# Attention scores as products over 128 rows, with zeros beside each head's queries

## The chip, the cores and the metric

The kernel runs on one core of a Trainium2 chip. Its engines work side by side and meet at semaphores: TensorE (PE in the profile; PEld is its weight load), VectorE (DVE), ScalarE (ACT), GpSimd (POOL), and SyncE (SP), which issues most transfers. The metric is the device time of one execution in microseconds (us); before the change the median of three runs is 1227.53 us (1225.55 to 1228.27).

## The reference

Attention with 32 of 576 scores kept per row, then a routed mixture of eight experts, then a last pair of layers with a leaky activation. The change touches only the first line of the attention:

```python
# q, k, v: 4 batches x 8 heads x 576 rows x 64
scores = scale * np.matmul(q, k.transpose(0, 1, 3, 2))
kth = np.partition(scores, -32, axis=-1)[..., -32:-31]
scores = np.where(scores >= kth, scores, -1000000000.0)
attn = softmax(scores)                    # rows of 576, 32 of them not zero
x = np.matmul(attn, v)                    # then experts and the last layers
```

## The kernel before

The attention takes the first 520 us or so. Heads are worked in 16 pairs (4 batches x 4), and a pair in nine tiles of 128 query rows: jobs j = 0 to 3 are the first 512 rows of the first head, 4 to 7 those of the second, and job 8 holds the last 64 rows of both. With all inputs at two heads of 64 columns side by side, a transposed tile `qk` has the first head on partitions 0 to 63 and the second on 64 to 127, 576 columns of q and 576 of k.

`tile_scores` multiplies a tile of queries (the weights, `qs`) with all 576 keys in two products of 288 columns, each of which TensorE runs as two matmuls (f32), so four per tile. For jobs 0 to 7 queries and keys are the 64 partitions of one head. For job 8 the queries are `qm`, 128 x 128, with the first head's last rows in the upper left quarter, the second head's in the lower right, and zeros elsewhere; the product then runs over all 128 partitions and yields 64 rows of each head.

The tiles go through a software pipeline, written out by hand in `ORDER`: in step i the kernel issues the transposes of tile i-6 (`st_transpose`, into `pt`), the product of tile i+1 (`st_scores`, into the only `s`), and the weighted sum of tile i-7 (`st_out`, into `po`) on TensorE; the evacuation of the transposes (`pT`), the copy of the scores out of `s` (`st_copy`, into one of seven `ss` buffers), the signs of tile i-1 against a threshold (`st_sign1`, `sg`, two buffers) and the exponential of tile i-2 on ScalarE; seven block maxima and the selection of the largest on VectorE; z = scores x signs (`st_z`, two buffers) and the mask (`st_mask`, L288 and L289, `pen`, four buffers) on GpSimd. VectorE reads z two steps after GpSimd made it. Every engine works its own list strictly in order.

While a pair is worked, the next one is prepared in the steps with j = 1, 3 and 5: `prep` transposes 96 rows at a time into a bank of `pt`, `prep_copy` copies 384 columns to `qk` on ScalarE, and after the second copy SP places the two quarters of `qm` by two transfers. For the very first pair `prep_all` does all three at once, before anything else can run. After a batch's last pair VectorE and TensorE route its rows to experts, and some steps later GpSimd scatters them with five indirect transfers (L751); after the last batch the expert weights, whose loading starts near the end of the attention, are multiplied.

Of the kernel before, what the change touches and what calls it, by code (L numbers as in the profile page):

```python
# [12 lines left out]
F32 = mybir.dt.float32  # L13
F32R = mybir.dt.float32r
BF = mybir.dt.bfloat16
I32 = mybir.dt.int32
AF = mybir.ActivationFunctionType
# [4 lines left out]
P = 128  # L22
B, H, S, D = 4, 8, 576, 64
# [3 lines left out]
CK = 116  # L27
NCK = 5
HALF = S // 2
# [16 lines left out]
class Job:  # L46


    def __init__(self, n, b, hp, j, st):
        self.n, self.b, self.hp, self.j, self.st = n, b, hp, j, st  # L50
        self.pre = None

    t = property(lambda self: self.st[self.b * NPAIR + self.hp])
# [3 lines left out]
class Attention:  # L57
    def __init__(self, ctx, tc, q, k, v, sb, ident):
        self.tc, self.nc = tc, tc.nc
        self.q, self.k, self.v = q, k, v  # L60
        self.ident = ident
        nc = self.nc
        self.wk = ctx.enter_context(tc.tile_pool(name="attn", bufs=2))
        self.ps = ctx.enter_context(tc.tile_pool(name="attn_ps", bufs=1, space=PSUM))
        one = ctx.enter_context(tc.tile_pool(name="attn_one", bufs=1))

        self.new_pt1()
        self.new_po()
        self.new_s()

        self.bank = self.ps.tile([P, 512], F32, name="own")
        self.taken = 0
        self.vt = []
        for i in range(3):
            t = one.tile([CK, NCK, 2, D + 1], F32, name=f"vt{i}")
            nc.gpsimd.memset(t, 0.0)
            nc.gpsimd.memset(t[:, :, :, D:D + 1], 1.0)
            self.vt.append(t)
        self.qm = []
        for i in range(2):  # L80
            t = one.tile([P, P], F32, name=f"qm{i}")
            nc.gpsimd.memset(t, 0.0)
            self.qm.append(t)
        self.scores, self.exps = [[one.tile([P, NCK * CK], F32, name=f"{nm}{i}") for i in range(n)]
                                  for nm, n in (("ss", 7), ("e", 5))]
        for t in self.scores + self.exps:
            nc.vector.memset(t[:, S:], 0.0)
        self.identb = one.tile([P, P], BF, name="identb")
        nc.vector.tensor_copy(self.identb, ident)
        vsel = one.tile([P, 9, 2], F32, name="vsel")  # L90
        nc.gpsimd.iota(vsel, pattern=[[2, 9], [1, 2]], base=S - 2 * TOP, channel_multiplier=0,
                       allow_small_or_imprecise_dtypes=True)
        nc.vector.memset(vsel[:, 0, 1:2], -float(S + 1))
        self.vsel = self.own(18).rearrange("p (a b) -> p a b", b=2)
        nc.vector.tensor_copy(self.vsel, vsel)
        self.rden = self.own(6)
        self.fac = self.own(2)
        self.least = self.own(3)
        nc.vector.memset(self.fac[:, 0:1], -0.125)
        nc.vector.memset(self.fac[:, 1:2], TINY)  # L100
        self.bad = sb.tile([P, 1], F32, name="bad")
        nc.vector.memset(self.bad, 0.0)
        self.per = NPAIR * 9
# [41 lines left out]
    def prep(self, t, g):  # L145

        if g == 0:
            t["qk"] = self.wk.tile([P, 2 * S], F32, name="qk", bufs=2)
        pt = self.ps.tile([P, 4, P], F32, name="pt0", bufs=2)
        pt = pt.rearrange("p a b -> p (a b)")[:, :384]  # L150
        for r in range(4):
            i, c = divmod(4 * g + r, 6)
            self.nc.tensor.transpose(pt[:, r * 96:(r + 1) * 96],  # L153
                                     t["qn" if i == 0 else "kn"][:, c].rearrange("p h d -> p (h d)"),
                                     self.ident[:96, :96])
        t["pp"] = pt

    def prep_copy(self, t, g):
        self.nc.scalar.activation(t["qk"][:, g * 384:(g + 1) * 384], t["pp"], AF.Copy)
        if g == 1:  # L160
            t["qm"] = self.qm[t["i"] % 2]
            for h in range(2):
                hs = slice(h * D, (h + 1) * D)
                self.nc.sync.dma_start(t["qm"][hs, hs], t["qk"][hs, S - D:S])

    def tile_scores(self, t, j):
        nc = self.nc
        s = self.new_s()
        h, c0 = divmod(j, 4)
        hs = slice(h * D, (h + 1) * D) if j < 8 else slice(0, P)  # L170
        qs = t["qk"][hs, c0 * P:(c0 + 1) * P] if j < 8 else t["qm"]
        for g in range(2):
            nc.tensor.matmul(s[:, g, :HALF], qs, t["qk"][hs, S + g * HALF:S + (g + 1) * HALF], start=True, stop=True)  # L173
        return s

    def st_scores(self, T):
# [73 lines left out]

    def new_pen(self, T):

        T.pen = self.wk.tile([P, NCK, CK + 4], BF, name="pen", bufs=4)[:, :, :CK]
        return T.pen

    def st_sign2(self, T):
# [6 lines left out]

    def st_sign1(self, T):
        nc, wk = self.nc, self.wk
        T.sg = wk.tile([P, S], F32, name="sg", bufs=2)
        T.c1 = wk.tile([P, 1], F32, name="c1", bufs=5)
        nc.scalar.activation(T.sg, T.ss, AF.Sign, bias=T.w[:, 23:24], scale=-ABOVE, accum_out=T.c1)  # L268

# [4 lines left out]

    def st_z(self, T):
        nc, wk = self.nc, self.wk
        T.z = wk.tile([P, S], F32, name="z", bufs=2)
        eng = nc.vector if T.n >= self.n - self.LASTZ else nc.gpsimd
        eng.tensor_tensor(T.z, T.ss, T.sg, op=OP.mult)  # L279

# [100 lines left out]
    def prep_all(self, t):  # L381
        for g in range(3):
            self.prep(t, g)
            self.prep_copy(t, g)

    def tiles(self, jobs, first, pair_done, batch_done, drain):

# [67 lines left out]
E, FF, FF2, DM = 8, 1024, 2048, H * D  # L455
# [20 lines left out]
class Router:  # L476
# [160 lines left out]
    def batch_done(self, b):  # L637

        nc, wk = self.nc, self.wk
        xs = [(P, self.xb[b][:, j]) for j in range(4)] + [(TAIL, self.xt[b][:, :])]  # L640
        n, t0 = BT, b * BT
# [5 lines left out]
        g, rr = self.narrow  # L647
        lx = new("lg", E)
        ss, r, m, fm = new("ss"), new("rn"), new("mrow"), new("fm")
# [51 lines left out]

        def square(t):
            k, x = xs[t]
            d = self.att.wk.tile([P, S], F32, name="sg", bufs=2)[:k, :DM]
            if t < 2:
                v.scalar_tensor_tensor(d, x[:, :DM], 1.0, x[:, :DM], op0=OP.mult, op1=OP.mult, accum_out=ss[:k, t:t + 1])
            else:
                nc.scalar.activation(d, x[:, :DM], AF.Square, accum_out=ss[:k, t:t + 1])
# [18 lines left out]
        if b == B - 1:  # L727
            low = [lambda f=f: self.low_half(f) for f in range(AHEAD)]
            ahead = lambda at: [lambda f=f: self.ahead(f) for f in range(AHEAD) if AT[f] == at]
            steps += [lambda t=t: square(t) for t in range(4)] + [low[f] for f in range(AHEAD) if AT[f] == 0] + ahead(1) + [  # L730
                lambda: self.last_dots(3), numbers] + ahead(2) + [last_copies, root] + first + [
                counts] + [low[f] for f in range(AHEAD) if AT[f] == 1] + norm + [exps] + ahead(3) + [
                low[f] for f in range(AHEAD) if AT[f] == 2] + [place]
            steps += [x for y in zip(where, sums) for x in y] + [low[f] for f in range(AHEAD) if AT[f] == 3]
        else:
            for t in range(n):
                steps += [("st_transpose", lambda t=t: tile_dots(t)), ("late", lambda t=t: tile_copy(t)),
                          ("late", lambda t=t: tile_norm(t))]
            mixed = [x for y in zip(where, norm) for x in y]
            steps += first + [NEXT, root, ("st_transpose", counts), ("late", place), NEXT] + mixed + [  # L740
                NEXT, exps, NEXT] + sums[:2] + [lambda: (gates(), numbers())]
# [904 lines left out]
```

## Time and profile before

| what | value |
|---|---|
| median of three runs | 1227.53 us |
| profiled execution, device time | 1226.84 us |
| its span | 1225.0 us |
| TensorE busy | 1192.3 us (97%) |
| VectorE, ScalarE, GpSimd busy | 834.1, 689.4, 684.1 us |
| mean granted clock of TensorE | 0.988 of full speed |

The span is what the profile shows of that execution, from its first to its last instruction. Busy time is the union of an engine's instructions; since they overlap at their ends, the start of one instruction to the start of the next says what it holds the engine for. "Idle before" names the event that ended an engine's idle time; "issue" is time for which nothing that the profile shows was waited for.

### The profile page before, as it was taken

To read this page: it belongs to the slowest core of one execution; us is meant where nothing else is said; L and a number is where in the kernel's file an instruction comes from. 1 tells how busy PE (TensorE), PEld (TensorE's weight loads), DVE (VectorE), ACT (ScalarE), POOL (GpSimd) and SP (SyncE) were. 2 spreads that over 40 slices of the span, in tenths; PEclk is the share of its full clock that TensorE was granted. 3 is DMA by queue.
4 is the path that set the end of the run, shared out by engine and by line. 5 is a ranking of instruction groups with operands and counts; after the bars stand their busy time and mean duration, and the time that the engine had idled before them with its cause. 6 is when DMAs were issued, how large, how long until landed. Compare 5 with 4: busy or idle time off the path is not lost.

```text
span 1225.0 us, 24804 instructions
## 1 busy us (share of the span) xinstructions
PE 1192.3 (97%) x8273; PEld 1059.4 (86%) x8273; DVE 834.1 (68%) x3636; ACT 689.4 (56%) x1475; POOL 684.1 (56%) x731
## 2 busy tenths in 40 slices
PE   7999999999999999998999999989999999999996
PEld 4888888888888888898999999979898898998995
DVE  5888888988798889866555566667657664454440
ACT  5899988999799979853544555522323222122120
POOL 4777777988789767951434345445335352333331
PEclk9999999999999999988999999989999999999999
DMA  4333222222222110438877787342232122222211
GB/s 134 96 102 101 57 56 55 83 69 56 56 73 54 33 32 14 149 111 172 211 202 217 187 240 234 112 133 84 69 118 73 54 67 70 78 61 76 73 42 55
DMA packets 121775, 121.24 MB, mean 99 GB/s; under 512 B 73454, under 2 KB 91374, under 8 KB 121638
## 3 DMA queue, kind: packets, MB, share of 16 engines
q1 hardware_dynamic: 118198, 109.58, 32.5%
q0 software_dynamic: 2912, 9.46, 2.1%
q8 instruction: 67, 1.10, 0.4%
q14 instruction: 70, 0.57, 0.2%
q10 hardware_dynamic: 528, 0.52, 0.1%
HBM read 84.58 MB, written 33.92 MB: 97 GB/s over the span
## 4 chain that ended last, share of the span: by engine, by line
PE 94%; DMA 2%; DVE 2%; ACT 1%; issue 1%; POOL 0%; SPq 0%; POOLq 0%; DVEq 0%
PE po L333 14%; PE s L173 14%; PE mm L1023 12%; PE mm L1024 12%; PE mm L1022 12%; PE pt L310 6%; PE mm L1245 5%; PE mm L1244 5%; PE mm L1243 5%; PE pt L312 2%; PE pt L153 2%; PE pt L616 1%; DMA yt<-y 1%; PE pt L596 1%; PE xt L1014 1%
## 5 line engine op out<-in xcount | busy, mean ns | idle before, releaser
L195 DVE MAX8 cand<-ss 128x8 f32<-128x82 f32 (+1 forms) x1008 | 233.3, 232 | 59.7 <-ACT ss L185 59.3
L1023 PE MATMUL mm<-xT,wt 128*128 128x256 f32 (+7 forms) x852 | 248.9, 292 | 4.4 <-DVE xT L1017 4.3
L1022 PE MATMUL mm<-xT,wt 128*128 128x256 f32 (+7 forms) x852 | 247.6, 291 | 5.5 <-ACT xT L1188 5.5
L279 POOL TENSOR_TENSOR z<-ss,sg 128x576 f32<-128x576 f32 x143 | 201.8, 1412 | 91.1 <-ACT sg L268 75.6
L1024 PE MATMUL mm<-xT,wt 128*128 128x256 f32 (+7 forms) x852 | 248.2, 291 | 0.0
L333 PEld LDWEIGHTS po<-vt,pT 116*128 116x128 f32 x1440 | 174.1, 190 | 32.4 <-issue 23.9
L333 PE MATMUL po<-vt,pT 116*128 116x130 f32 x1440 | 194.8, 281 | 0.6 <-ACT pc L365 0.6
L1228 POOL TENSOR_TENSOR hT<-xr,hT 128x256 fp32r<-128x256 f32 x144 | 106.3, 743 | 152.4 <-ACT hT L1227 145.5
L1227 ACT ACTIVATE hT<-xr 128x256 fp32r<-128x256 f32 x144 | 59.0, 416 | 200.9 <-DVE xr L1224 194.0
L173 PE MATMUL s<-qk 64*128 64x288 f32 x512 | 166.3, 447 | 3.8 <-ACT ss L185 3.2
L1022 PEld LDWEIGHTS mm<-xT,wt 128*128 128x128 f32 x852 | 162.9, 191 | 6.5 <-ACT xT L1188 5.7
L1023 PEld LDWEIGHTS mm<-xT,wt 128*128 128x128 f32 x852 | 163.2, 191 | 5.6 <-DVE xT L1017 4.5
L1024 PEld LDWEIGHTS mm<-xT,wt 128*128 128x128 f32 x852 | 163.8, 192 | 0.0
L310 PE MATMUL pt<-ident,e 128*116 128x128 f32 x720 | 129.5, 275 | 1.2 <-POOL e L285 1.2
L1223 DVE TENSOR_SCALAR xr<-mm,alpha 128x256 f32<-128x256 f32 x144 | 69.4, 482 | 84.3 <-PE mm L1024 83.3
L185 ACT ACTIVATE ss<-s 128x576 f32<-128x576 f32 x144 | 94.2, 654 | 55.8 <-PE s L173 53.7
L173 PEld LDWEIGHTS s<-qk 64*128 64x128 f32 x512 | 89.6, 194 | 39.7 <-ACT ss L185 7.0
L947 POOL TENSOR_TENSOR wt<-raw,wt 128x1024 fp32r<-128x1024 f32 x29 | 76.3, 2633 | 83.0 <-ACT wt L946 78.3
L268 ACT ACTIVATE sg<-ss,w 128x576 f32<-128x576 f32 x144 | 111.7, 776 | 0.3 <-DVE w L208 0.2
L273 ACT ACTIVATE e<-ss,sm 128x576 f32<-128x576 f32 x144 | 111.2, 772 | 0.0
L217 DVE MAX8 w<-z 128x8 f32<-128x576 f32 x144 | 106.8, 742 | 2.3 <-POOL z L279 1.8
L312 PE MATMUL pt<-identb,pen 128*116 128x128 bf16 x560 | 99.5, 220 | 0.2 <-POOL pen L289 0.2
(254 smaller groups left out, 2666.7 us busy)
## 6 DMA issues: line engine op xcount, KB each, us to landing
raw<-in_moe_w SPq DMA_DIRECT2D x60, 512.0 KB
xr<-yt SPq DMA_DIRECT2D x17, 512.0 KB
xs<-zeros SPq DMA_DIRECT2D x8, 1028.0 KB
raw<-in_moe_w_in SPq DMA_DIRECT2D x16, 512.0 KB
raw<-in_moe_w_out SPq DMA_DIRECT2D x16, 512.0 KB
yt<-zeros SPq DMA_DIRECT2D x8, 704.0 KB
rows<-in_q SPq DMA_DIRECT2D x32, 144.0 KB
rows<-in_k SPq DMA_DIRECT2D x32, 144.0 KB
```

What stands on the lines that cost most here:

```text
L173: nc.tensor.matmul(s[:, g, :HALF], qs, t["qk"][hs, S + g * HALF:S + (g + 1) * HALF], start=True, stop=True)
L195: blocks.append(lambda i=i: nc.vector.max(A.cand[:, i], A.ss[:, i * BW:(i + 1) * BW if i + 1 < KB else S]))
L217: fin = [lambda: nc.vector.max(C.w[:, 24:32], C.z), lambda: nc.vector.scalar_tensor_tensor(scr, self.vsel, C.c1, C.w[:, 23:32, None].to_br ...
L268: nc.scalar.activation(T.sg, T.ss, AF.Sign, bias=T.w[:, 23:24], scale=-ABOVE, accum_out=T.c1)
L273: nc.scalar.activation(T.e[:, :S], T.ss, AF.Exp, bias=T.sm[:, 0:1], scale=0.125)
L279: eng.tensor_tensor(T.z, T.ss, T.sg, op=OP.mult)
L310: nc.tensor.matmul(o, e, self.ident, is_transpose=True, start=True, stop=not pen)
L312: nc.tensor.matmul(o, T.pen[:, c], self.identb, start=False, stop=True)
L333: nc.tensor.matmul(po[:, i:i + 2, :], T.pT[:, c], rhs, start=(c == 0), stop=(c == NCK - 1))
L1022: nc.tensor.matmul(ps, wh, xh, start=first, stop=False)
L1023: nc.tensor.matmul(ps, wh, xl, start=False, stop=False)
L1024: nc.tensor.matmul(ps, wl, xh, start=False, stop=last)
```

## The change

The queries are laid out with zeros. `qz` (two buffers, 128 x 1152, cleared once) holds in columns 0 to 575 the first head's queries on partitions 0 to 63, and further right the second head's on 64 to 127, its last 64 rows in columns 576 to 639 and the other 512 from column 640 on. Any 128 columns that a job takes are then one head's queries with zeros beside them, or, for job 8 (columns 512 to 639), the two quarters. All products of scores run over 128 partitions, against a `kt` with the keys of both heads. q goes to a staging tile `qt` first, from which three transfers fill `qz`; for the first pair (`direct`) ScalarE copies the first head's part straight from the transposes, and VectorE the second head's. z overwrites the signs, `sg` has three buffers in place of two and two, `ss` has six in place of seven, and `pen` three in place of four.

```diff
@@ -76,13 +76,15 @@
             nc.gpsimd.memset(t, 0.0)
             nc.gpsimd.memset(t[:, :, :, D:D + 1], 1.0)
             self.vt.append(t)
-        self.qm = []
+
+
+        self.qz = []
         for i in range(2):
-            t = one.tile([P, P], F32, name=f"qm{i}")
+            t = one.tile([P, 2 * S], F32, name=f"qz{i}")
             nc.gpsimd.memset(t, 0.0)
-            self.qm.append(t)
+            self.qz.append(t)
         self.scores, self.exps = [[one.tile([P, NCK * CK], F32, name=f"{nm}{i}") for i in range(n)]
-                                  for nm, n in (("ss", 7), ("e", 5))]
+                                  for nm, n in (("ss", 6), ("e", 5))]
         for t in self.scores + self.exps:
             nc.vector.memset(t[:, S:], 0.0)
         self.identb = one.tile([P, P], BF, name="identb")
@@ -145,7 +147,9 @@
     def prep(self, t, g):
 
         if g == 0:
-            t["qk"] = self.wk.tile([P, 2 * S], F32, name="qk", bufs=2)
+            t["q"] = self.wk.tile([P, S], F32, name="qt", bufs=1)
+            t["k"] = self.wk.tile([P, S], F32, name="kt", bufs=2)
+            t["qz"] = self.qz[t["i"] % 2]
         pt = self.ps.tile([P, 4, P], F32, name="pt0", bufs=2)
         pt = pt.rearrange("p a b -> p (a b)")[:, :384]
         for r in range(4):
@@ -155,22 +159,36 @@
                                      self.ident[:96, :96])
         t["pp"] = pt
 
-    def prep_copy(self, t, g):
-        self.nc.scalar.activation(t["qk"][:, g * 384:(g + 1) * 384], t["pp"], AF.Copy)
-        if g == 1:
-            t["qm"] = self.qm[t["i"] % 2]
-            for h in range(2):
-                hs = slice(h * D, (h + 1) * D)
-                self.nc.sync.dma_start(t["qm"][hs, hs], t["qk"][hs, S - D:S])
+    SECOND = ((0, S - D, S + D), (S - D, S, D))
+
+    def prep_copy(self, t, g, direct=False):
+        nc = self.nc
+        for x, o in (("q", 0), ("k", S)):
+            lo, hi = max(g * 384, o), min((g + 1) * 384, o + S)
+            if lo >= hi:
+                continue
+            src = t["pp"][:, lo - g * 384:hi - g * 384]
+            if x == "q" and direct:
+                nc.scalar.activation(t["qz"][:D, lo:hi], src[:D], AF.Copy)
+                for a, b, to in self.SECOND:
+                    a, b = max(a, lo), min(b, hi)
+                    if a < b:
+                        nc.vector.tensor_copy(t["qz"][D:, to + a:to + b], src[D:, a - lo:b - lo])
+            else:
+                nc.scalar.activation(t[x][:, lo - o:hi - o], src, AF.Copy)
+        if g == 1 and not direct:
+            nc.sync.dma_start(t["qz"][:D, :S], t["q"][:D])
+            for a, b, to in self.SECOND:
+                nc.sync.dma_start(t["qz"][D:, to + a:to + b], t["q"][D:, a:b])
 
     def tile_scores(self, t, j):
         nc = self.nc
         s = self.new_s()
         h, c0 = divmod(j, 4)
-        hs = slice(h * D, (h + 1) * D) if j < 8 else slice(0, P)
-        qs = t["qk"][hs, c0 * P:(c0 + 1) * P] if j < 8 else t["qm"]
+        q0 = c0 * P + h * (S + D) if j < 8 else S - D
+        qs = t["qz"][:, q0:q0 + P]
         for g in range(2):
-            nc.tensor.matmul(s[:, g, :HALF], qs, t["qk"][hs, S + g * HALF:S + (g + 1) * HALF], start=True, stop=True)
+            nc.tensor.matmul(s[:, g, :HALF], qs, t["k"][:, g * HALF:(g + 1) * HALF], start=True, stop=True)
         return s
 
     def st_scores(self, T):
@@ -250,7 +268,7 @@
 
     def new_pen(self, T):
 
-        T.pen = self.wk.tile([P, NCK, CK + 4], BF, name="pen", bufs=4)[:, :, :CK]
+        T.pen = self.wk.tile([P, NCK, CK + 4], BF, name="pen", bufs=3)[:, :, :CK]
         return T.pen
 
     def st_sign2(self, T):
@@ -263,7 +281,7 @@
 
     def st_sign1(self, T):
         nc, wk = self.nc, self.wk
-        T.sg = wk.tile([P, S], F32, name="sg", bufs=2)
+        T.sg = wk.tile([P, S], F32, name="sg", bufs=3)
         T.c1 = wk.tile([P, 1], F32, name="c1", bufs=5)
         nc.scalar.activation(T.sg, T.ss, AF.Sign, bias=T.w[:, 23:24], scale=-ABOVE, accum_out=T.c1)
 
@@ -274,7 +292,7 @@
 
     def st_z(self, T):
         nc, wk = self.nc, self.wk
-        T.z = wk.tile([P, S], F32, name="z", bufs=2)
+        T.z = T.sg
         eng = nc.vector if T.n >= self.n - self.LASTZ else nc.gpsimd
         eng.tensor_tensor(T.z, T.ss, T.sg, op=OP.mult)
 
@@ -381,7 +399,7 @@
     def prep_all(self, t):
         for g in range(3):
             self.prep(t, g)
-            self.prep_copy(t, g)
+            self.prep_copy(t, g, True)
 
     def tiles(self, jobs, first, pair_done, batch_done, drain):
 
@@ -701,7 +719,7 @@
 
         def square(t):
             k, x = xs[t]
-            d = self.att.wk.tile([P, S], F32, name="sg", bufs=2)[:k, :DM]
+            d = self.att.wk.tile([P, S], F32, name="sg", bufs=3)[:k, :DM]
             if t < 2:
                 v.scalar_tensor_tensor(d, x[:, :DM], 1.0, x[:, :DM], op0=OP.mult, op1=OP.mult, accum_out=ss[:k, t:t + 1])
             else:
```

Per engine the order of the tiles stays as it was. It changes in two places.

At the start, ScalarE's first rows before (the transposes of the first pair lie in three banks, `pt_154`, `pt_160`, `pt_168`):

```order
L159 ACT_TABLE_LOAD
L159 ACTIVATE qk<-pt_154 128x384 [waits PE_49]
L159 ACTIVATE qk<-pt_160 128x384 [waits PE_49]
L159 ACTIVATE qk<-pt_168 128x384 [waits PE_49]
L185 ACTIVATE ss_109<-s 128x576 [waits PE_49]
```

And after (the banks are now `pt_153`, `pt_160`, `pt_169`):

```order
L172 ACT_TABLE_LOAD [waits PE_49]
L172 ACTIVATE qz_105<-pt_153 64x384 [waits Pool_49]
L172 ACTIVATE qz_105<-pt_160 64x192 [waits PE_49]
L178 ACTIVATE kt<-pt_160 128x192 [waits DVE_49]
L178 ACTIVATE kt<-pt_169 128x384 [waits PE_49]
L203 ACTIVATE ss_109<-s 128x576 [waits PE_49]
```

There is one copy more, the wait for TensorE stands ahead of the table load, and the copy of k waits for VectorE. VectorE's rows in the same place, after:

```order
L95 MEMSET vsel 128x1 [waits Pool_49]
L97 COPY own<-vsel 128x18 [waits DVE_49]
L101 MEMSET own 128x1 [waits DVE_49]
L102 MEMSET own 128x1 [waits DVE_49]
L104 MEMSET bad 128x1
L176 COPY qz_105<-pt_153 64x384 [waits Activation_49]
L176 COPY qz_105<-pt_160 64x128 [waits Activation_49]
L176 COPY qz_105<-pt_160 64x64
L514 TENSOR_SCALAR rev<-iota 128x8 [waits Pool_49]
```

The three copies stand between the constants (`vsel`, which GpSimd makes after its clearings) and the rest; before, `rev` followed `bad` at once. On TensorE the third group of the first pair's transposes waits for these copies, where it waited for ScalarE's first copy:

```order
L157 MATMUL pt_160<-ident,rows 128x96 [waits DMAHW3_49,DMAHW2_49]
L157 MATMUL pt_160<-ident,rows 128x96
L157 MATMUL pt_169<-ident,rows 128x96 [waits DVE_49]
L157 MATMUL pt_169<-ident,rows 128x96 x3
L191 MATMUL s<-kt,qz_105 128x288 [waits Activation_49,Pool_49]
L191 MATMUL s<-kt,qz_105 128x288
```

In the preparation of each later pair, SP's rows before, with the loads of the pair after next behind them:

```order
L164 DMA qm_107<-qk 64x64 [waits DMAHW6_49,Activation_49]
L164 DMA qm_107<-qk 64x64 [waits DMAHW7_49]
L132 DMA rows<-in_q 96x6x64 [waits DMAHW0_49,PE_49]
L132 DMA rows<-in_q 96x6x64 [waits DMAHW1_49]
L132 DMA rows<-in_k 96x6x64 [waits DMAHW2_49]
```

And after:

```order
L180 DMA qz_107<-qt 64x576 [waits DMAHW4_49,Activation_49]
L182 DMA qz_107<-qt 64x512 [waits DMAHW5_49]
L182 DMA qz_107<-qt 64x64 [waits DMAHW6_49]
L134 DMA rows<-in_q 96x6x64 [waits DMAHW7_49,PE_49]
L134 DMA rows<-in_q 96x6x64 [waits DMAHW0_49]
```

Three transfers stand where two were, the first two of them with 576 and 512 columns in place of 64.

## Rows read from the trace of the kernel before

**Rows 1.** The page: busy time, the chain that ended last, one costly group.

```profile
PE 1192.3 (97%) x8273; PEld 1059.4 (86%) x8273; DVE 834.1 (68%) x3636; ACT 689.4 (56%) x1475; POOL 684.1 (56%) x731
...
PE 94%; DMA 2%; DVE 2%; ACT 1%; issue 1%; POOL 0%; SPq 0%; POOLq 0%; DVEq 0%
...
L217 DVE MAX8 w<-z 128x8 f32<-128x576 f32 x144 | 106.8, 742 | 2.3 <-POOL z L279 1.8
```

**Rows 2.** Stretches: length, then busy us of PE, PEld, DVE, ACT, POOL; clock; DMA.

```profile
66.68:97.04 30.36, 30.36 (x225) 25.07 (x224) 26.36 (x173) 27.96 (x63) 24.20 (x26) 1.00 0.37 102
...
224.00:258.00 34.00, 34.00 (x253) 28.32 (x252) 29.73 (x199) 31.46 (x71) 31.41 (x37) 1.00 0.32 92
...
465.00:505.00 40.00, 40.00 (x288) 32.57 (x289) 38.30 (x250) 36.74 (x82) 33.36 (x40) 1.00 0.28 102
```

**Rows 3.** Line 173, the scores: count, ns min/median/max, first and last start, form.

```profile
L173 PE MATMUL s<-qk x512: 402/403/847, 7.4 to 505.5; 64*128 64x288 f32 x171
...
L173 PE MATMUL s<-qk,qm x64: 406/406/848, 34.9 to 509.0; 128*128 128x288 f32 x64
```

**Rows 4.** TensorE in time, jobs 7, 8 and 0: start, us, instruction.

```profile
63.47 1.23 PE L173 MATMUL s<-qk 64*128 64x288 f32 x4
64.63 1.39 PE L333 MATMUL po<-vt,pT 116*128 116x130 f32 x10
65.85 0.27 PE L310 MATMUL pt<-ident,e 128*116 128x128 f32 x1
...
66.63 0.22 PE L312 MATMUL pt<-identb,pen 128*116 128x128 bf16 x1
66.68 1.19 PE L173 MATMUL s<-qk,qm 128*128 128x288 f32 x4
67.71 1.28 PE L333 MATMUL po<-vt,pT 116*128 116x130 f32 x10
68.83 0.27 PE L310 MATMUL pt<-ident,e 128*116 128x128 f32 x1
...
69.60 0.22 PE L312 MATMUL pt<-identb,pen 128*116 128x128 bf16 x1
69.75 1.23 PE L173 MATMUL s<-qk 64*128 64x288 f32 x4
```

**Rows 5.** Waits from 40 to 505 us: total, times, longest.

```profile
PEld po L333 <- issue: 23.5, 61, 0.4
```

**Rows 6.** All engines in time, 254 to 258 us.

```profile
254.48 0.75 POOL L288 TENSOR_SCALAR mg<-ss,nk 128x580 f32<-128x580 f32 x1
...
255.81 0.65 ACT L185 ACTIVATE ss<-s 128x576 f32<-128x576 f32 x1
...
257.12 0.76 ACT L273 ACTIVATE e<-ss,sm 128x576 f32<-128x576 f32 x1
...
257.78 0.58 ACT L317 ACTIVATE pT<-pt 116x512 f32<-116x512 f32 x1
```

**Rows 7.** All engines in time, the start.

```profile
0.82 1.28 ACT L159 ACT_TABLE_LOAD   x1 [0.82 <-PEq L1631]
...
2.82 0.64 POOL L76 MEMSET vt<- 116x650 f32 x1
...
3.56 0.35 POOL L82 MEMSET qm<- 128x128 f32 x2
...
4.73 0.06 DVE L102 MEMSET bad<- 128x1 f32 x1
...
5.15 0.49 ACT L159 ACTIVATE qk<-pt 128x384 f32<-128x384 f32 x1 [3.04 <-PE pt L153]
...
5.62 1.20 PE L153 MATMUL pt<-ident,rows 96*128 96x96 f32 x6 [0.18 <-DMA rows<-in_k]
...
7.39 2.28 PE L173 MATMUL s<-qk 64*128 64x288 f32 x4 [0.58 <-ACT qk L159]
```

**Rows 8.** SP's queue in time: the transfers that place the queries.

```profile
55.59 1.16 SPq L164 DMA_DIRECT2D qm<-qk  x2
```

## The prediction

> **What bounds the kernel now.** Read the page's busy shares and its chain of waits first [rows 1]: TensorE is busy for 97% of the span and makes up 94% of the chain that ends last. A busy TensorE need not be TensorE at its peak, so the next view is the stage that the change touches: the 30.36 us in which one pair of heads passes, from one product with `qm` (66.68 us) to the next (97.04 us) [rows 2]. There TensorE is without a gap, ScalarE has 27.96 us of work, VectorE 26.36 and GpSimd 24.20. TensorE sets the pace, but ScalarE stands only 2.40 us behind. Two other stretches of the same view have less room: the 34 us after a batch's routing (GpSimd 31.41 of 34), and the last 40 us of the attention (VectorE 38.30 of 40) [rows 2].
>
> Now TensorE alone, tile by tile. The kernel already holds both forms of the product: 512 matmuls on 64 rows and 64 on 128 rows, the latter with zeros beside each head's queries [rows 3]. One matmul of either takes the same time, 403 against 406 ns. What differs is what stands around it. Follow the starts in [rows 4]. A tile on 64 rows: product at 63.47, first weighted sum (`po`) at 64.63, first transpose (`pt`) at 65.85; that is 1.16 + 1.22 = 2.38 us. The tile on 128 rows: 66.68, 67.71, 68.83; that is 1.03 + 1.12 = 2.15 us. And the product starts 0.05 us after the last transpose when it is on 128 rows (66.63 to 66.68), 0.15 us when on 64 (69.60 to 69.75). In all 0.23 + 0.10 = 0.33 us per tile. The waits name the same spot: the weight load of `po` is held 0.4 us, 61 times, by "issue", that is by nothing that another engine does [rows 5].
>
> **The gain on TensorE.** The 512 matmuls are 128 tiles of four. In the first pair a matmul takes up to 847 ns (the other form is still at 848 in the first pair's ninth tile, from 34.9 us) [rows 3], and there each product waits for the copy of the one before, so I count nothing for its eight tiles. 120 x 0.33 = 39.6 us. A pair would take 30.36 - 8 x 0.33 = 27.72 us.
>
> **What ScalarE gives back.** Its work in a pair is 27.96 us as shown, 0.24 more than TensorE would then need; over the 12 pairs without routing that is 2.9 us. But busy time counts an instruction's tail: e starts at 257.12 and takes 0.76, yet the next instruction starts at 257.78, after 0.66 [rows 6]. Where ScalarE stops to wait, some 8 times a pair, that tenth is no work; 27.96 - 0.8 = 27.2 us, below TensorE's 27.72. A new cost comes on top: of the three copies of q and k in a pair the second is split in two, for which the row's tail of 0.10 us is an upper end (1.5 us in 15 pairs). I take 1.4 us lost for all this; the ends are 0 and 4.4.
>
> **What GpSimd gives back.** After the routing of batch 0 and of batch 1 GpSimd also scatters rows and is full for some ten tiles [rows 2]. TensorE would pass these 10 x 0.33 = 3.3 us sooner; GpSimd can't. One score buffer less bites here: ScalarE's copy of scores into a buffer must follow GpSimd's last read of the tile six back, not seven. In [rows 6] that read (L288) ends at 254.48 + 0.75 = 255.23 and the copy that would wait for it starts at 255.81: 0.58 us of room. Beyond it ScalarE waits, and behind that copy on its queue are the signs and the exponential, for which GpSimd's next z and then VectorE wait. TensorE needs the copy only for its next product: in [rows 4] a product ends at 66.68 + 1.19 = 67.87, a copy takes 0.65 [rows 6], the next product starts at 69.75, so TensorE has 1.23 us of its own, 0.9 at the new pace. 3.3 - 0.6 - 0.9 = 1.8 us per batch, 3.6 for two; the ends are 1.8 (VectorE's and ScalarE's room absorbs half) and 5.4 (TensorE's slack is already used up).
>
> **What VectorE gives back.** From 465 to 505 us VectorE has 1.7 us left [rows 2], while 11 tiles on 64 rows would save 3.6 us. At least 1.9 us stay lost; I take 2.1 (ends 1.9 and 3.6).
>
> **The start.** Two things make the first product later. ScalarE's table load (1.28 us at 0.82, when nothing waited) now has the wait for TensorE's first transposes ahead of it, so it starts where the first copy started, at 5.15, and the copy (0.49) ends near 6.92 [rows 7]. And VectorE has three new copies of head 1's queries. GpSimd clears two `qz` of 1152 columns instead of two `qm` of 128: 650 columns take 0.64 us and the two of 128 together 0.35 [rows 7], which makes 0.9 ns a column, 1.1 us for one `qz` and 1.8 us more for both; VectorE's constants, which wait for GpSimd's next result and ended at 4.79, end at 6.6. So the first of VectorE's copies starts at 6.92, behind ScalarE's of the same bank. For its 384 columns I estimate 0.5 us from the maximum over 576 columns in 742 ns [rows 1]: 7.4. TensorE's third group of four transposes reuses that bank and now waits for VectorE. Before, six transposes from 5.62 on (the last two of the second group and the third group; 1.20 us) and a copy led to the first product at 7.39 [rows 7]: 1.77 us, without the first two 1.37. 7.4 + 1.4 = 8.8: 1.4 us later; the ends are 0.5 (the copies overlap what waits anyway) and 2.6 (they all follow each other).
>
> On this term the Trainium skill has a rule of its own ("PSUM — Partial Sum Buffer", section "PSUM bank collisions raise a hardware error"): two engines must not access one bank and quadrant at once, two reads included. The order of the changed kernel agrees so far that ScalarE's copy of k waits for VectorE's of q out of the same bank; no run here yet shows its time. By the rule alone the copies of the two engines follow each other, the start's term would be at its upper end of 2.6 us and the forecast at 1198 us.
>
> **What costs nothing.** The transfers that place the queries, three instead of two per pair, are issued at 55.59 us and the next pair's first product needs them at 69.75 us [rows 4, 8]: 14 us of cover (13 at the new pace), and SP has nothing queued there. If that cover went, each pair's first product would wait for it. Signs overwritten in place: the third buffer comes free when VectorE has read z of three tiles before, and ScalarE already waits for a later result of VectorE (the thresholds) before it writes signs. The `pen` buffers, three instead of four, are read by TensorE at least one tile before they are written again. After the attention the instructions are the same; I let them start earlier and last as long.
>
> **The sum.** 39.6 - 1.4 - 3.6 - 2.1 - 1.4 = 31.1 us. The profiled execution took 1226.84 us: 1195.7. The median of the runs is 0.7 us above it: 1196 us.
>
> **The rivals.**
> 1. *All of it arrives.* GpSimd's and VectorE's lateness is absorbed by the buffers and ScalarE keeps up. For it: in an ordinary pair GpSimd has 24.20 and VectorE 26.36 us for 27.72. Against it: VectorE's 38.30 of 40 us. 1227.5 - 39.6 + 1.4 = 1189 us.
> 2. *ScalarE becomes the bound.* If the 2.40 us that it is free in a pair are half latency that stays, a pair takes 27.96 + 1.2 = 29.2 us and gains 1.2, not 2.6. 14 pairs x 1.2 = 17 us: 1210 us. For it: 92% busy; against it: its overlapping tails.
> 3. *The transfers are late (slower).* Place: the first product of each pair, which now reads `qz` in place of the copy itself. Up to 13 us from issue to landing cost nothing; each microsecond more costs one per pair, and at 15.6 us the gain of 2.6 is gone. With 18 us a pair loses 5 and gains 2.6: 1227.5 + 14 x 2.4 = 1261 us. Against it: two such transfers are issued within 1.16 us [rows 8], and the queue is empty behind them.
> 4. *The gaps are not the rows'.* The tile that is better differs also in being the ninth of its pair. Then only the start changes: 1228 us. Against it: all around the product is alike in both tiles, the same weighted sums behind it and the same transposes ahead of it [rows 4].
>
> **How the numbers follow.** My forecast reaches, with all ends good or all bad, from 1191 to 1204 us and has 0.62; rival 1 has 0.15, rival 2 0.18, rival 3 0.03, rival 4 0.02. The range of 1187 to 1207 us takes in the forecast, most of rival 1 and the better part of rival 2. A difference under 0.2% (2.5 us) can't be told from none here: faster 0.95, same 0.02, slower 0.03.
>
> **What would show it.** In the changed profile the four matmuls of a product should start within 1.03 us of the next `po`, `po` should last 1.12 us until the transposes, and the 0.4 us of "issue" before `po` should be gone. An ordinary pair should take 27.7 to 27.9 us, the pair after a routing about 1.8 more than that, with ScalarE's score copy waiting for GpSimd. The first product should start near 8.8 us. If the pair takes over 29 us while TensorE has gaps, rival 2 holds; if TensorE's gaps stand ahead of each pair's first product, rival 3; if the rhythm around the product is still 1.16 and 1.22, rival 4.

## The result and the profile after

| what | before | after |
|---|---|---|
| median of the runs | 1227.9 us (4 runs) | 1197.85 us (1195.94 to 1198.48, 4 runs) |
| profiled execution, its span | 1226.84, 1225.0 us | 1197.81, 1195.9 us |
| first product of the first pair | 7.39 us | 9.20 us |
| ninth product of the first pair, of the last | 34.89, 508.26 us | 33.95, 479.39 us |

The ratio is 0.9756 (95% interval 0.9739 to 0.9773); 1196 us was predicted. The last product of the attention starts 28.87 us sooner, of 29.1 us of span: what follows takes as long as it did.

The page of the changed kernel, where [rows 1] stood: busy time, the chain that ended last, and VectorE's maximum over z.

```profile
PE 1151.7 (96%) x8273; PEld 1064.5 (89%) x8273; DVE 832.4 (70%) x3638; ACT 683.3 (57%) x1491; POOL 686.0 (57%) x731
...
PE 84%; DVE 7%; POOL 3%; ACT 2%; DMA 2%; issue 1%; POOLq 0%; SPq 0%; ACTq 0%; DVEq 0%
...
L235 DVE MAX8 w<-sg 128x8 f32<-128x576 f32 x144 | 106.8, 742 | 4.6 <-POOL sg L297 3.6
```

TensorE's busy time fell by 40.6 us, the span by 29.1: the 11.5 us between them are idle time of TensorE that the kernel before did not have. In the chain VectorE and GpSimd have 7% and 3% now, where it was 2% and 0%. The stretches that answer to [rows 2] (length, then busy us of PE, PEld, DVE, ACT, POOL, clock, DMA): an ordinary pair, the 34 us after the routing of batch 0, the last 40 us of the attention.

```profile
63.19:90.90 27.71, 27.71 (x225) 25.68 (x224) 26.12 (x173) 27.47 (x64) 24.19 (x26) 1.00 0.45 122
207.00:241.00 34.00, 32.25 (x254) 28.57 (x253) 30.42 (x199) 31.19 (x71) 31.43 (x38) 1.00 0.38 106
440.00:480.00 40.00, 36.73 (x283) 32.74 (x283) 37.81 (x244) 35.66 (x81) 34.84 (x41) 1.00 0.31 112
```

The ordinary pair has no gap on TensorE; the other two have 1.75 and 3.27 us of them. Around a product, where [rows 3 and 4] stood:

```profile
L191 PE MATMUL s<-kt,qz x576: 405/407/850, 9.2 to 480.2; 128*128 128x288 f32 x192
```

```profile
63.13 0.22 PE L330 MATMUL pt<-identb,pen 128*116 128x128 bf16 x1
63.19 1.19 PE L191 MATMUL s<-kt,qz 128*128 128x288 f32 x4
64.21 1.28 PE L351 MATMUL po<-vt,pT 116*128 116x130 f32 x10
65.33 0.27 PE L328 MATMUL pt<-ident,e 128*116 128x128 f32 x1
```

From the product to `po` it is 1.02 us, from `po` to `pt` 1.12, from the last transpose to the product 0.06. Of the 0.4 us of "issue" ahead of `po` [rows 5] nothing is left. What TensorE and ScalarE wait for instead, from 40 to 480 us (total, times, longest):

```profile
ACT ss L203 <- POOL mg L306: 9.1, 9, 1.7
...
PEld L330 <- POOL pen L307: 7.4, 9, 1.4
PE pt L330 <- POOL pen L307: 5.4, 6, 1.2
...
POOL mx L387 <- DMA xs<-xb,slot: 1.3, 1, 1.3
```

One such place in time, which [rows 6] had without a wait (start, us, engine, instruction, in brackets the idle time before it and what ended it):

```profile
223.71 1.19 PE L191 MATMUL s<-kt,qz 128*128 128x288 f32 x4
224.32 0.09 POOL L768 MEMSET spacer<- 1x1 f32 x1
224.57 1.05 POOL L769 DMA_INDIRECT xs<-xb,slot  x1 [0.16 <-issue]
...
225.71 0.74 POOL L306 TENSOR_SCALAR mg<-ss,nk 128x580 f32<-128x580 f32 x1
...
226.48 0.65 ACT L203 ACTIVATE ss<-s 128x576 f32<-128x576 f32 x1 [1.60 <-POOL mg L306]
226.54 0.67 POOL L307 TENSOR_SCALAR pen<-mg 128x580 bf16<-128x580 f32 x1
...
227.26 0.27 PE L330 MATMUL pt<-identb,pen 128*116 128x128 bf16 x1 [0.78 <-POOL pen L307]
227.29 1.41 POOL L297 TENSOR_TENSOR sg<-ss,sg 128x576 f32<-128x576 f32 x1
```

A scatter of batch 0 (L769) stands ahead of a mask. Two engines then wait for GpSimd at once: ScalarE for a score buffer, and TensorE for the mask itself. The product after it starts at 228.03, 4.32 us after the one shown; the same tile of the next pair, without a scatter, takes 3.33.

The start, where [rows 7] stood, and the transfers of [rows 8]:

```profile
3.56 2.06 POOL L84 MEMSET qz<- 128x1152 f32 x2
5.20 1.28 ACT L172 ACT_TABLE_LOAD   x1 [5.20 <-PE pt L157]
6.49 0.70 ACT L172 ACTIVATE qz<-pt 64x384 f32<-64x384 f32 x2
7.01 0.91 DVE L176 COPY qz<-pt 64x384 f32<-64x384 f32 x3 [0.51 <-ACT qz L172]
7.62 0.90 PE L157 MATMUL pt<-ident,rows 96*128 96x96 f32 x4 [1.58 <-DVE qz L176]
7.95 0.33 ACT L178 ACTIVATE kt<-pt 128x192 f32<-128x192 f32 x1 [0.76 <-DVE qz L176]
8.56 0.49 ACT L178 ACTIVATE kt<-pt 128x384 f32<-128x384 f32 x1 [0.28 <-PE pt L157]
```

```profile
53.09 0.51 SPq L180 DMA_DIRECT2D qz<-qt  x1
53.70 1.19 SPq L182 DMA_DIRECT2D qz<-qt  x2
```

### The profile page after: what moved, and what is told of

It reads as the page before. It is cut to its first block, busy times and chain, and to the rows that moved or that the text cites. A ratio compares the mean times of both kernels' runs of the same rounds, so it can differ in the third digit from the quotient of the medians.

```text
span 1195.9 us, 24814 instructions
## 1 busy us (share of the span) xinstructions
PE 1151.7 (96%) x8273; PEld 1064.5 (89%) x8273; DVE 832.4 (70%) x3638; ACT 683.3 (57%) x1491; POOL 686.0 (57%) x731
## 4 chain that ended last, share of the span: by engine, by line
PE 84%; DVE 7%; POOL 3%; ACT 2%; DMA 2%; issue 1%; POOLq 0%; SPq 0%; ACTq 0%; DVEq 0%
PE mm L1041 12%; PE mm L1042 12%; PE mm L1040 12%; PE po L351 10%; PE s L191 10%; PE mm L1263 6%; PE mm L1262 6%; PE mm L1261 6%; PE pt L328 5%; PE pt L330 2%; DVE cand L213 2%; DVE w L235 1%; PE pt L157 1%; POOL sg L297 1%; PE pt L634 1%
## 5 line engine op out<-in xcount | busy, mean ns | idle before, releaser
L297 POOL TENSOR_TENSOR sg<-ss,sg 128x576 f32<-128x576 f32 x143 | 201.7, 1411 | 59.4 <-ACT sg L286 46.2
L351 PEld LDWEIGHTS po<-vt,pT 116*128 116x128 f32 x1440 | 179.0, 190 | 13.6 <-ACT pc L383 4.6
L351 PE MATMUL po<-vt,pT 116*128 116x130 f32 x1440 | 186.5, 275 | 1.9 <-ACT pc L383 1.8
L191 PE MATMUL s<-kt,qz 128*128 128x288 f32 x576 | 177.3, 432 | 4.1 <-ACT ss L203 3.1
L191 PEld LDWEIGHTS s<-kt,qz 128*128 128x128 f32 x576 | 101.8, 197 | 25.0 <-ACT ss L203 7.5
L235 DVE MAX8 w<-sg 128x8 f32<-128x576 f32 x144 | 106.8, 742 | 4.6 <-POOL sg L297 3.6
```

The lines of the kernel that those rows point to most:

```text
L191: nc.tensor.matmul(s[:, g, :HALF], qs, t["k"][:, g * HALF:(g + 1) * HALF], start=True, stop=True)
L235: fin = [lambda: nc.vector.max(C.w[:, 24:32], C.z), lambda: nc.vector.scalar_tensor_tensor(scr, self.vsel, C.c1, C.w[:, 23:32, None].to_br ...
L351: nc.tensor.matmul(po[:, i:i + 2, :], T.pT[:, c], rhs, start=(c == 0), stop=(c == NCK - 1))
```

## The experiments

Lengths of stretches of the attention, in us, from the start of one pair's ninth product to that of another's (pair 0: from its first product to its ninth). With 0.33 us less on each of the eight tiles, a pair would be 2.64 us shorter than before. Pairs 9 and 13, between the last columns, hold the routing of batches 1 and 2. The edits are cut to their main lines.

| kernel | median | first product | pair 0 | pair 1 | 2 to 5 | 6 to 8 (scatters of batch 0) | 10 to 12 (batch 1) | 14, 15 (batch 2) |
|---|---|---|---|---|---|---|---|---|
| before | 1227.9 | 7.39 | 27.50 | 31.79 | 125.35 | 92.85 | 92.83 | 62.04 |
| after | 1197.85 | 9.20 | 24.76 | 29.23 | 114.67 | 88.25 | 89.26 | 61.04 |
| 1: 64 rows again | 1230.17 | 9.31 | 27.52 | 32.54 | 125.35 | 92.84 | 92.83 | 62.09 |
| 2: pair 0 on 64 rows | 1202.12 | 9.26 | 27.53 | 29.22 | 114.67 | 88.29 | 88.49 | 61.04 |
| 3: seven ss, four pen | 1196.31 | 9.17 | 23.81 | 29.23 | 114.68 | 88.28 | 88.75 | 61.08 |
| 4: a scatter every third tile | 1198.83 | 9.24 | 24.29 | 29.71 | 114.66 | 87.80 | 88.44 | 61.04 |
| 5: scatters where GpSimd has no mask | 1192.58 | 9.25 | 24.28 | 29.71 | 114.67 | 85.40 | 85.92 | 61.07 |
| 6: one step more | 1195.84 | 9.18 | 23.78 | 27.87 | 113.90 | 88.33 | 88.09 | 59.18 |
| 7: two masks on VectorE | 1193.49 | 9.27 | 24.75 | 29.26 | 114.67 | 88.33 | 89.10 | 58.06 |
| 8: the start | 1196.82 | 8.04 | 24.29 | 29.45 | 114.65 | 88.25 | 88.95 | 61.06 |
| 9: 5, 7 and 8 together | 1188.54 | 8.17 | 23.68 | 28.98 | 114.69 | 85.38 | 86.22 | 58.08 |

Against 0.33 us a tile the changed kernel lost 88.25 - (92.85 - 7.92) = 3.3 us after batch 0, 4.3 after batch 1 and 61.04 - (62.04 - 5.28) = 4.3 in the last two pairs: 11.9 us.

The medians tell a difference of a microsecond or two less well than the stretches do. In the profiled executions of kernels with the same instructions behind the attention, what follows its last product took from 713.3 us (run 7) to 721.1 (run 4), 716.8 before and 716.5 after the change.

**1. The products on 64 rows again** (the keys too), all else as changed.

```diff
-        qs = t["qz"][:, q0:q0 + P]
+        hs = slice(h * D, (h + 1) * D) if j < 8 else slice(0, P)
+        qs = t["qz"][hs, q0:q0 + P]
```

> The changed kernel, with one thing put back: jobs 0 to 7 multiply only the 64 partitions of their head (same qz, same kt, same transfers, same buffers); job 8 stays on 128. Theory (the gain is the step between products on 64 rows and the 128-row work around them): s to po goes back from 1.03 to 1.16 us, po to pt from 1.12 to 1.22, the 0.4 us of issue before po return, an ordinary pair takes 30.36 us again, the waits for GpSimd after the routings shrink to those of before, and the time is 1227.9 + 1.8 (the start) = 1229.7 us, or about 1226 if the clock still rises at 31 us in the first pair. Rival (the gain comes from what else changed: staging of q, buffers, layout of keys): pair 27.7, time within 2 us of 1197.9.

Measured: 1230.17 us, ratio to before 1.0017 (1.0007 to 1.0027). TensorE of that kernel in time, jobs 7 and 8:

```profile
66.15 1.23 PE L192 MATMUL s<-kt,qz 64*128 64x288 f32 x4
67.31 1.39 PE L352 MATMUL po<-vt,pT 116*128 116x130 f32 x10
68.54 0.28 PE L329 MATMUL pt<-ident,e 128*116 128x128 f32 x1
...
69.37 1.19 PE L192 MATMUL s<-kt,qz 128*128 128x288 f32 x4
70.39 1.28 PE L352 MATMUL po<-vt,pT 116*128 116x130 f32 x10
71.51 0.27 PE L329 MATMUL pt<-ident,e 128*116 128x128 f32 x1
```

1.16 and 1.23 us are back around the product on 64 rows, 1.02 and 1.12 stand around the one on 128. From pair 2 on every stretch has the length of before; the first product stays late, and pair 1 is 0.75 us longer, since the clock rises later there (run 2). The whole gain, and all that was given back in the attention, hang on the rows.

**2. The first pair alone on 64 rows** (`if t["i"] == 0 and j < 8` in the line above).

> The changed kernel, but the first pair alone multiplies on 64 partitions (jobs 0 to 7). In it the matmuls last 687 ns until about 31 us in the changed kernel and until about 38.9 us in the kernel before, then 407. Theory (the products on 128 rows bring the higher clock sooner): the long matmuls last until about 39 us again and the time rises by some 3 to 4 us to about 1201. Rival (the later start or the other gaps between instructions bring it): the rise stays near 31 us and only the tiles after it lose 0.33 us each, so below 1199 us.

Measured: 1202.12 us, 4.3 more than the changed kernel by the medians. In the traces the first pair takes 2.77 us more and the last product comes 2.1 later; the rest is no part of the attention. Products of the first pair in time: before, after, this kernel.

```profile
29.94 2.29 PE L173 MATMUL s<-qk 64*128 64x288 f32 x4
34.89 2.29 PE L173 MATMUL s<-qk,qm 128*128 128x288 f32 x4
39.93 1.23 PE L173 MATMUL s<-qk 64*128 64x288 f32 x4
```

```profile
27.46 2.29 PE L191 MATMUL s<-kt,qz 128*128 128x288 f32 x4 [0.87 <-ACT ss L203]
31.13 1.14 PE L191 MATMUL s<-kt,qz 128*128 128x288 f32 x4
```

```profile
31.84 2.29 PE L192 MATMUL s<-kt,qz 64*128 64x288 f32 x4
36.78 2.29 PE L192 MATMUL s<-kt,qz 128*128 128x288 f32 x4
41.66 1.19 PE L192 MATMUL s<-kt,qz 128*128 128x288 f32 x4
```

Four matmuls take 2.29 us at the lower level of TensorE's clock (1.2 GHz) and about 1.2 at the higher (2.4). With 64 rows in the first pair the record of the clock rises at 38.9 us (before), 42.4 (run 1) and 40.6 (here), with 128 rows at 31.0 (after). Of the profiled executions on record, all ten with 128 rows in that pair show the first rise at 31.2 us or sooner, all three with 64 at 38.9 or later. The theory stands; what it is about the rows that brings the clock up stays open.

**3. The old buffers:** seven `ss`, four `pen` (room by lending a `qz` buffer to the last loads in place of one raw tile).

```diff
-                                  for nm, n in (("ss", 6), ("e", 5))]
+                                  for nm, n in (("ss", 7), ("e", 5))]
-name="pen", bufs=3
+name="pen", bufs=4
```

> The changed kernel with the buffers of before: seven ss and four pen (room comes from lending a qz buffer in place of one raw tile to the last loads). Losses against 0.33 us per tile now: about 3.3 us after the routing of batch 0, 4.3 after batch 1, 4.3 in the last stretch. Theory of the prediction (the copy of scores waits for a buffer that GpSimd still reads): the 9.1 us of ACT ss waiting for GpSimd nearly vanish, at least 3.6 us come back, time 1194 or less. Rival (GpSimd is late with the data itself: TensorE's mask transposes wait for pen, VectorE for z): the wait moves from ss to those, and the time stays within 1 us of 1197.9.

Measured: 1196.31 us, ratio to before 0.974 (0.9724 to 0.9756), not to be told from the changed kernel's. The waits of this kernel, 40 to 480 us:

```profile
PEld L330 <- POOL pen L307: 7.9, 9, 1.4
...
PE pt L330 <- POOL pen L307: 5.9, 6, 1.2
```

And from 207 to 256 us, behind the routing of batch 0:

```profile
DVE w L235 <- POOL sg L297: 3.3, 4, 1.1
```

The 9.1 us of ScalarE waiting for a mask (`ss` for `mg`) are gone, TensorE's wait for the masks is as it was (7.4 and 5.4 us), and the stretches of batches 0 and 2 keep their length (that of batch 1 is 0.5 us shorter, but it differs among the kernels that change nothing there: 89.26, 88.49 and 88.95 us in the table, with the 1.3 us in which GpSimd waits for a scatter's transfer). The 1.5 us by which the median is lower, more than the rival's 1 us, are no sign of the buffers: in the profiled execution the last product comes 1.4 us sooner, 0.95 of it in the first pair, where the clock rose sooner (19.7 us), and 0.5 in batch 1. The prediction's mechanism, the missing score buffer, falls; the rival stands.

**4. A scatter every third tile** after batches 0 and 1 (here and in run 5 two small tiles of a batch have a third buffer, since they are held longer).

```diff
-GAP = (2, 2, 2, 0)
+GAP = (3, 3, 2, 0)
```

> The changed kernel with the scatters of batches 0 and 1 every third tile in place of every second (and three buffers for the two small tiles of a batch, which are then held longer); batch 2 as it was. Theory (GpSimd has more work than time while it scatters: 5.4 us of masks and z plus 1.45 per scatter in 6.2 us of two tiles): per three tiles it has 8.1 + 1.45 in 9.2, so nearly all of the 7.6 us lost after batches 0 and 1 shrinks to 2 or less, time about 1192 to 1193. Rival (what is lost comes from the routing itself or from waits for transfers, not from GpSimd's load): no change, 1197 to 1198.

Measured: 1198.83 us. The pairs 6 to 8 and the routing pair behind them are 87.80 + 31.89 in place of 88.25 + 31.50 us, the same sum; batch 1 wins 0.4 by the same count. My theory of too much work on average falls: more time between scatters alone wins nothing. In this kernel the tile from 223.26 to 227.55 has a scatter ahead of a mask and takes 4.29 us; so does the one from 252.50 to 256.75, with 4.25.

**5. The scatters of batches 0 and 1 in the steps in which VectorE makes the mask.**

```diff
-            steps += [NEXT] * GAP[b] + [lambda i=i, k=k, x=x: self.scatter(t0 + i, x, k)]
+            steps += ([NEXT, ("wait", lambda: (self.att.now - 4) % 9 in (3, 8))] if b < 2 else [NEXT] * GAP[b])
+            steps += [lambda i=i, k=k, x=x: self.scatter(t0 + i, x, k)]
```

> The changed kernel with the scatters of batches 0 and 1 in the steps in which GpSimd has no mask to make (two of nine; VectorE makes it there), so that each stands between two z and none between z and the mask of the same step; with three buffers for the two small tiles of a batch. Five scatters then take some 22 tiles; spacing them by three tiles without regard to the masks had won nothing. Theory (GpSimd has time enough in sum, but a mask behind a scatter reaches TensorE's transposes of the same step 0.8 to 1.2 us late): the tiles of 4.2 to 5.0 us after batches 0 and 1 vanish, at most 1.5 of 7.6 us stay lost, time 1191 to 1192.5. Rival (each scatter costs TensorE its share wherever it stands, since GpSimd has no time left): as many us lost as now, 1197 to 1199.

Measured: 1192.58 us, ratio to before 0.9711 (0.9691 to 0.9731). GpSimd and TensorE at the place that was shown above:

```profile
223.27 1.19 PE L191 MATMUL s<-kt,qz 128*128 128x288 f32 x4
223.57 0.75 POOL L306 TENSOR_SCALAR mg<-ss,nk 128x580 f32<-128x580 f32 x1
224.41 0.67 POOL L307 TENSOR_SCALAR pen<-mg 128x580 bf16<-128x580 f32 x1
225.16 1.41 POOL L297 TENSOR_TENSOR sg<-ss,sg 128x576 f32<-128x576 f32 x1
...
226.51 0.09 POOL L770 MEMSET spacer<- 1x1 f32 x1
...
226.61 0.70 PE L191 MATMUL s<-kt,qz 128*128 128x288 f32 x2
226.76 1.05 POOL L771 DMA_INDIRECT xs<-xb,slot  x1 [0.17 <-issue]
```

The scatter stands between two z; the tile takes 3.34 us. The last product comes 5.3 us sooner (474.08), 2.85 and 3.3 in the two stretches, less 0.4 in each routing pair behind them. The scatters also stand further apart here, four or five tiles in place of two; that this is not the cause is seen in run 4, where the tiles with a scatter ahead of a mask were as long at three. The theory stands: it is the step that has to hold both a scatter (1.4 us with its spacer) and a mask (1.6) beside z (1.4), 4.4 us for a tile of 3.0.

**6. A step more between mask and transposes,** with the old buffers.

```diff
-(("st_norm", 8), ("st_transpose", 6), ("st_sign2", 4), ("st_evac_a", 6),
+(("st_norm", 9), ("st_transpose", 7), ("st_sign2", 4), ("st_evac_a", 7),
```

> The changed kernel with one step more between making a mask and reading it: transposes, their evacuation, weighted sums and what follows one step later, with seven ss and four pen as in the run with the old buffers. Theory (the masks are late by latency, not by GpSimd's load): a tile more of room, 3.1 us, takes up a scatter's 1.4 us; of 11.9 us lost in the three stretches at most 4 stay; the pipeline is a step longer at its end, which costs 1 to 3 us: 1189 to 1193. Rival (GpSimd's load is the bound there): the losses stay at 10 us or more and the longer end comes on top: 1197 to 1200.

Measured: 1195.84 us. The routing is a tile later here against the products, so a stretch behind it is counted with the next routing pair: pairs 6 to 9 take 118.84 us in place of 119.75 (119.78 in run 3, with the same buffers), pairs 10 to 13 take 118.60 in place of 120.75 (120.25 in run 3), pairs 14 and 15 win 1.9. From 207 to 256 us this kernel waits:

```profile
DVE w L235 <- POOL sg L297: 3.0, 3, 1.2
ACT e L291 <- DVE sm L228: 1.5, 2, 0.9
```

No transpose waits for a mask now. What is left is VectorE, which reads z in order and waits for those behind the scatters; it did so in run 3 as well, for 3.3 us, and in the changed kernel for 1.1. The theory is half right: 0.9, 2.1 and 1.9 us come back, so that of 11.9 some 7 stay lost, where it allowed 4. The time is between the theory's and the rival's. The last product comes 8.0 us sooner than in the changed kernel, but what follows it takes 6.2 us longer, with the pipeline one step longer at its end; 1 to 3 had been expected.

**7. Two masks of the last stretch on VectorE,** those of tiles 132 and 136, which stand behind scatters of batch 2.

```diff
-        return self.KINDS[T.j] if T.n < self.n - 3 else 0
+        return self.KINDS[T.j] if T.n < self.n - 3 and T.n not in (132, 136) else 0
```

> The changed kernel with the masks of two tiles of the last two pairs (numbers 132 and 136 of 144, the ones that stand right behind a scatter of batch 2 on GpSimd) made by VectorE, as it makes those of jobs 3 and 8; 0.82 us each there in place of 1.5 on GpSimd. It tells apart who holds the last stretch, of which the prediction said VectorE. Theory (GpSimd again: masks behind scatters are late): the two tiles of 4.24 and 4.32 us shrink to about 3.0 to 3.3, 2 to 2.5 us come back, time 1195.5. Rival (VectorE has no time left in that stretch): two masks more cost up to 1.6 us more there, time 1198 to 1199.5.

Measured: 1193.49 us, ratio to before 0.972 (0.97 to 0.9741); pairs 14 and 15 take 3.0 us less. The last 40 us:

```profile
440.00:480.00 40.00, 39.05 (x310) 35.56 (x309) 39.91 (x254) 38.68 (x87) 35.02 (x41) 1.00 0.32 112
```

VectorE is busy for 39.91 of 40 us and the stretch is shorter all the same. In the changed kernel GpSimd held it, not VectorE. Of the 4.3 us lost there 1.3 stay; 0.8 of them is one wait of TensorE's weighted sum for ScalarE's copy of the one before (`po` for `pc`), which the changed kernel has too. The rest of the 4.4 us between the medians is no part of the attention and stays unexplained; four runs spread over 4.3 us.

**8. The start:** the table load without a wait ahead of it, the second `qz` cleared later.

```diff
+            warm = pools[1].tile([P, 1], F32, name="warm")
+            nc.scalar.activation(warm, ident[:, :1], AF.Copy)
             att.prep_all(st[0])
+            nc.gpsimd.memset(att.qz[1], 0.0)
```

> The changed kernel with two edits at the start: a one-column activation ahead of the first pair's copies, so that the table load has no wait for TensorE ahead of it, and the second qz cleared after the first pair's copies are issued, not ahead of them. The first product starts at 9.20 us in the changed kernel, 7.39 before it. Theory (table load 1.28 us and the clearing of 1.0 us hold VectorE's and ScalarE's copies): it starts at 7.4 to 7.8 us, and the time falls by about 1.6 to 1196.2. Rival (the copies of the two engines out of one bank follow each other, and that chain is what is long): it starts after 8.5 us and the time stays within 0.7 us of 1197.9.

Measured: the first product at 8.04 us, between the two; 1196.82 us. The table load and the clearing together made up 1.16 of the 1.81 us (the run does not part them). The 0.65 that stay go, by its trace, to the copies in turn: ScalarE's copy of k waits 0.50 us for VectorE's of q.

**9. What wins, together.** The start and the scatters:

> The changed kernel with the start's two edits and the scatters of batches 0 and 1 in the steps without a mask on GpSimd, buffers as in the changed kernel. If the gains add: 1197.9 - 1.1 - 5.3 = 1191.5. If the start's microsecond is taken up elsewhere in the first pair: 1192.6.

Measured: 1192.81 us: the start's microsecond is not seen in the medians. The last product comes 2.0 us sooner than in run 5, what follows it takes 3.0 longer. The same with the old buffers:

> The changed kernel with the start's two edits, the scatters of batches 0 and 1 in the steps without a mask on GpSimd, and seven ss and four pen. If the three gains add: 1197.9 - 1.1 - 5.3 and at most 1.5 for the buffers: 1190 to 1191.5. If buffers matter only where masks are late, none of the 1.5: as the kernel without them, 1191.5.

Measured: 1192.13 us, no difference. And the start, the scatters and the two masks:

> The start's two edits, the scatters of batches 0 and 1 in the steps without a mask on GpSimd, and the masks of tiles 132 and 136 on VectorE. By the theory that late masks behind scatters make up the loss in all three stretches: 1191.5 - 2.3 = 1189.2. By the rival (VectorE is the bound in the last stretch): 1191.5 or more.

Measured: 1188.54 us (1186.47 to 1189.78), ratio to before 0.9672 (0.9651 to 0.9693): faster than both kernels. Pairs 6 to 15 win 8.2 us on the changed kernel; 3.5 stay lost against 0.33 us a tile, and what holds those is only in part known (run 7).

## Why the prediction was right, and where not

The time was 2 us off; of the steps some were exact, and the errors of others cancelled. That it came so close is luck in part: without the 2.75 us of the first pair, which it did not have, it would have been 4.6 off.

- **TensorE's 39.6 us: right, cause and size.** The pair was put at 27.72 us; it takes 27.71. Run 1 shows that it is the rows. The Trainium skill ("TensorEngine Tiling (Array Packing)", section "Key Properties") says that a change of the tiling mode drains TensorE; that fits 0.23 us after a product on 64 rows and 0.10 ahead of it, for which the page has no figure. No run shows whether it is this drain or something else about the rows.
- **The first pair "counted at nothing": wrong by 2.75 us** (24.76 for 27.50). That each product waits there for a copy was right, but the clock rose at 31.0 us in place of 38.9, and with 64 rows in that pair its 27.5 us are back (run 2).
- **ScalarE gives back 1.4: nothing,** its lower end. With 27.47 us of work it keeps up with a pair of 27.71, without a gap on TensorE; rival 2 is out.
- **GpSimd gives back 3.6 through the score buffers: 7.6, and by another way.** The place and the engine were right, the step "ScalarE's copy must follow GpSimd's read of the tile six back" is what failed. That wait came (9.1 us), yet with seven buffers it goes and the time stays (run 3). TensorE waits for the mask. I had looked at GpSimd's sum in a stretch; what counts is the single step with scatter, mask and z. At 3.37 us a tile it found room in the steps beside it, and TensorE's waits for masks came to 0.2 us; at 3.08 it does not. More steps between scatters (run 4) don't bring the time back, a later reader (run 6) a part of it, a step without a mask (run 5) 2.45 and 2.95 us with the routing pairs counted in.
- **VectorE gives back 2.1 at the end: 4.3, and 3.0 of it not VectorE.** The scatters of batch 2 stand in that stretch too. 38.30 of 40 us busy was read as a bound; run 7 gave that engine more work and won 3.0. What holds the other 1.3 stays open but for one wait (0.8 us).
- **The start's 1.4: 1.81.** The first product came at 9.20 for 8.8. All three parts of the chain were seen, and run 8 sizes two of them together. The rule of the Trainium skill that the prediction names ("PSUM — Partial Sum Buffer", section "PSUM bank collisions raise a hardware error") is for one bank and quadrant, and the prediction carried it too far: ScalarE's and VectorE's copies of q read partitions 0 to 63 and 64 to 127, different quadrants. It covers the 0.76 us in which ScalarE's copy of k, on all 128 partitions, waited for VectorE's copies; the 0.51 us that VectorE waited for ScalarE's it does not ask for. The term stayed below the 2.6 us given for it, since the third transposes overlap the last of VectorE's copies.
- **No cost from transfers, signs and `pen`: right.** The transfers are issued at 53.09 us, and at 66.16 the next pair's first product waits for nothing; run 3 bounds the buffers.

The sum by the trace: 39.6 + 2.75 - 1.81 - 11.9 = 28.6, of 28.9 measured. The errors were -4.0 (GpSimd), -2.2 (the end), -0.4 (the start), +2.75 (first pair) and +1.4 (ScalarE).

## What to carry to other kernels

When the pace gets faster, look at the steps that exceed the new pace by themselves, not at an engine's sum over a stretch: an irregular instruction costs what its own step has too much, and moving it to a step with room wins more than buffers do. A wait that shows (a buffer) may be a companion of the one that counts; give the buffer back and see. An engine that is busy for 96% of a stretch is not thereby shown to be the bound.

## What the runs showed of the hardware beyond that

- The clock of the first pair rose sooner with products on 128 rows, half of them on zeros: in the changed kernel at 31.0 us, though TensorE had a gap of 0.87 us that ended at 27.46; before the change it had no gap from 25.83 us on, and the rise came at 38.9. In the other kernels with 128 rows in pair 0 the first rise was between 17.7 and 31.2 us, in four of them with a fall again at 24.6 to 26.5 us and a second rise by 32.4; what sets it within that span stays open.
- A matmul of 288 columns takes 403 ns on 64 rows and 407 on 128: zeros beside the queries cost 4 ns in the product itself.
